# Half of the edge masks of query tiles 0 and 3 moved into free contraction rows of the second score product

## The chip, the cores and the metric

The kernel runs on one core of a Trainium2 chip. The metric is the device time of one execution in microseconds. Every time below is from runs of the same inputs; the profile is one execution taken by the hardware profiler.

## The reference

One transformer block with modulated layer norms, S = 2048 tokens of D = 448, H = 16 heads of 28, all in fp32:

```python
mod = (silu(c) @ w_mod).reshape(1, 6, 1, 448)          # sa, ca, ga, sb, cb, gb
h = layernorm(x) * (1 + ca) + sa
qkv = h @ wqkv                                          # per head q, k, v: [2048, 28]
d = idx[:, None] - idx[None, :]
scores = where((d >= 0) & (d < 256), q @ k.T * 28 ** -0.5, -1e9)
x = x + ga * (softmax(scores) @ v @ wo)
h = layernorm(x) * (1 + cb) + sb
t = h @ w1 + b1                                         # 448 -> 1792
x = x + gb * ((t * tanh(softplus(t))) @ w2)
```

What matters here is the attention: a query sees its own position and the 255 before it. Cut into tiles of 128, a query tile sees three key tiles: its own (there the keys after the query are masked, the "diag" triangle), the one before it (nothing is masked), and the one before that (there the keys 256 or more before the query are masked, the "far" triangle).

## The kernel before, in words

fp32 products are made from fp32r parts: a value is split into a rounded high part and a rest, and products run over high x high, high x low and low x high. Two stages follow each other: attention with all that feeds it (to about 406 us), then the feed-forward part.

**Groups, heads, units.** The tokens are cut into NG = 4 groups of GT = 512 queries (four query tiles t = 0 to 3, and with the 256 keys before them six key tiles jj = 0 to 5). Each group has 16 heads, so there are 64 heads i = 16 g + h in order, and each head has three units b = 0, 1, 2, so 192 units u = 3 i + b. A unit packs score blocks into one PSUM bank of 512 columns, as BLOCKS says: unit 0 has (key tile 0, query tile 0) and (key tile 2, query tiles 0 to 2); unit 1 has (1; 0, 1) and (4; 2, 3); unit 2 has (3; 1 to 3) and (5; 3). Group 0 has no keys before it and leaves out the blocks of jj = 0 and 1.

**Two score products.** For each head a first one, A (line 683), makes scores with queries as rows, from 84 contraction rows (28 dimensions x 3 split parts), and DVE takes the masked row maximum of each query (line 685). M2 (lines 689 to 698) turns the maxima of a pair of heads into rows with a transpose, splits them into two fp32r parts in the tile mr, and two DMAs put these into rows 84 and 85 of the query tile Q2. The key tile K3 has -1 in these rows, so that the second score product, B (line 713), with keys as rows, yields scores less the maximum straight from 86 contraction rows. B runs once per block of a unit; the 128-column block or the two equal blocks come behind the wider one.

**Masks.** On top of B's products in the same bank lie mask products (line 724): the 128x128 identity (identr, bf16) times columns of fdmask (bf16, 256 columns: far triangle of -2^100 in 0 to 127, diag triangle in 128 to 255). Where a far tile is followed at once by a diag tile, one product of 256 columns does both. In groups 1 to 3 unit 0 so has one of 256 (columns 0 to 255) and one of 128 (columns 384 to 511), unit 1 one of 256 (128 to 383), unit 2 one of 128 (0 to 127) and one of 256 (256 to 511). In group 0 there are four of 128 and one of 256 in the three units together.

**Behind the scores.** ACT makes P = exp(scale x) twice, in fp32 and in fp32r (lines 727, 728), POOL their difference Pl (line 735; for the last five units POOL and DVE half each), and PE sums Ph and Pl times v into one PSUM bank per head (line 745). ACT takes the sums out (EV), PE transposes them (E), and E2, E3 divide.

**What sets the order.** The order on every engine is the program's own, written by the loop over u: in step u come PV(u - 3) with Pl, B(u), the subtraction SP(u - 1), one first product A of the head three ahead, and filler products, the next group's projections and the last group's output projection (line 315), as many as RATE allows per step; PV(u - 2) with Ph is last. Engines run their own queues in order and wait on semaphores. Loads of a head's q and k (L, lines 472 to 479) are issued two heads ahead of its first product A. K3 has six tiles (NK) and Q2 three tiles of two heads (NQ = 6), reused in turn.

**Deferred DMAs.** All DMAs but one go through SP's queue. Stores and loads of the filler work stand in a list, later, from which the loop pops one in two of three steps; flush() issues all that is in it. The generator that sums the modulation weights (gen_wm_sum) puts four loads in the list, one in each of its steps, and calls flush() two steps after the last.

**At the start**, POOL sets constants: -1 in rows 64 to 85 of the key tiles (k3_tile, lines 149 to 152), the identity, the float mask of A, and fdf, the fp32 form of fdmask, which ACT copies to bf16 (line 512). The last key tile and the query tiles 1 and 2 are made later, in the pool att, when the first staging pool is closed.

Of the kernel before, what the change touches and what calls it, by code (L numbers as in the profile page):

```python
# [8 lines left out]
F32 = mybir.dt.float32  # L9
F32R = mybir.dt.float32r  # L10
BF16 = mybir.dt.bfloat16
AF = mybir.ActivationFunctionType
ALU = mybir.AluOpType

S, D, F, H, DH, W = 2048, 448, 1792, 16, 28, 256
NG, GT = 4, 512
# [4 lines left out]
NQ, NK, NV, LEAD = 6, 6, 10, 3  # L21
# [30 lines left out]
def adaln_block(ctx: ExitStack, tc: tile.TileContext, x, wqkv, wo, w1, b1, w2, c, w_mod, out):  # L52
    nc = tc.nc
    PE, ACT, DVE, POOL = nc.tensor, nc.scalar, nc.vector, nc.gpsimd
# [3 lines left out]
    def dma(o, i):  # L58
        nc.sync.dma_start(o, i)

    def pool(name, side="left", space=None):
        kw = {} if space is None else {"space": space}
        cm = tc.tile_pool(name=name, bufs=1, reuse_waits="tile", side=side, **kw)
        st = ExitStack()
        return st.enter_context(cm), st
# [7 lines left out]
    kq, kq_s = pool("kq")  # L73
# [18 lines left out]
    def bank(tag, bufs, name):  # L92
        return PS[0].tile([128, 512], F32, name=name, tag=tag, bufs=bufs)
# [18 lines left out]
    for k in range(4):  # L112
        wmf = st0.tile([128, 2 * D], F32, name=f"wm01_{k}")
        t = wmf[0:112]
# [10 lines left out]
    two = wqkv[:, 128:1152].rearrange("r (a n) -> r a n", n=512)[:, :, 0:256]  # L125
    for part in range(3):
        for ci in range(4):
            r0, r1 = ci * 128, min(ci * 128 + 128, D)
            for h in ((slice(0, 128),) if ci < 3 else (slice(0, 64), slice(64, 128))):
                t = wqs[ci][h]  # L130
# [9 lines left out]
    ident = cst.tile([128, 128], F32, name="ident")  # L140
# [6 lines left out]
    K3 = []  # L147

    def k3_tile(pl, i):
        t = pl.tile([86, GT + W], F32R, name=f"k3_{i}")  # L150
        POOL.memset(t[64:86, :].bitcast(F32), -1.0)
        K3.append(t)

    for i in range(NK - 1):
        k3_tile(kq, i)
    identr = kq.tile([128, 128], BF16, name="identr")
    fdmask = kq.tile([128, 256], BF16, name="fdmask")
    mask = kq.tile([128, 384], F32, name="mask")
    DVE.tensor_copy(identr, ident)
    POOL.memset(mask, 0.0)  # L160
# [1 line left out]
                       channel_multiplier=-1)  # L162
    POOL.affine_select(mask, mask, pattern=[[-1, 384]], compare_op=ALU.is_ge, fill=NEG, base=W,
                       channel_multiplier=1)
# [136 lines left out]
    def finish():  # L301
        while pipe.items:
            yield

    def drain(*gs):
        for g in gs:
            for _ in g:
                pipe.step()
# [14 lines left out]
    later = []  # L323
    PARTS = {}

    def flush():
        while later:
            later.pop(0)()
# [130 lines left out]
    for v in V:  # L459
        POOL.memset(v[:, :, 28:29].bitcast(F32), 1.0)  # L460
        POOL.memset(v[:, :, 29:32].bitcast(F32), 0.0)
    fdf = wmf[:, 0:256]
    POOL.memset(fdf[:, 0:256], 0.0)
    POOL.affine_select(fdf[:, 0:128], fdf[:, 0:128], pattern=[[-1, 128]], compare_op=ALU.is_ge, fill=-2.0 ** 100,
                       base=-1, channel_multiplier=1)
    POOL.affine_select(fdf[:, 128:256], fdf[:, 128:256], pattern=[[1, 128]], compare_op=ALU.is_ge,
                       fill=-2.0 ** 100, base=0, channel_multiplier=-1)


    Q2 = [kq.tile([86, 2, GT], F32R, name="q2_0")]  # L470

    def L(i):
        g, h = divmod(i, H)
        q, k = Q2[i % NQ // 2][:, i % 2], K3[i % NK]
        f0, f1 = h * DH, D + h * DH
# [5 lines left out]
    def split_cols(c0, c1, engs):  # L481
        for ci in range(4):
            if engs[ci]:
                split_hi(wqs[ci][:, c0:c1], wq3[:, ci, c0:c1], ACT)
        for ci in range(4):
            if engs[ci]:
                split_lo(wqs[ci][:, c0:c1], wq3[:, ci, c0:c1], wql[:, min(ci, 2), c0:c1], ci, engs[ci])
# [21 lines left out]
    first_tiles([(4, bank("sA", 2, "qk0_4"))])  # L509
    flush()  # L510
    split_cols(*QCOLS[2], (POOL, POOL, DVE, DVE))
    ACT.activation(fdmask, fdf, AF.Copy)
    st0_s.close()
    att, att_s = pool("att")
    Q2 += [att.tile([86, 2, GT], F32R, name=f"q2_{i}") for i in range(1, NQ // 2)]
    Q3 = [Q2[i // 2][:, i % 2] for i in range(NQ)]
    k3_tile(att, NK - 1)

    O2 = []
    for i in range(2):  # L520
        t = att.tile([128, GT], F32, name=f"o2_{i}")
# [167 lines left out]
    def M2(pr):  # L689
        p = bank("tr", 1, f"mt{pr}")  # L690
        PE.transpose(p[0:8, 0:128], mx[pr].rearrange("p a t -> p (a t)"), ident)
        r = att.tile([8, 2, 128], F32R, name=f"mr{pr}", tag="mr", bufs=2)
        DVE.tensor_copy(r[:, 0], p[0:8, 0:128])
        DVE.tensor_tensor(r[:, 1], p[0:8, 0:128], r[:, 0].bitcast(F32), op=ALU.subtract)
        for i in range(2):
            dma(Q2[pr % (NQ // 2)][84 + i:85 + i].bitcast(F32).rearrange("o a (t n) -> o (a t) n", t=4),
                r[:, i].bitcast(F32))

    def units(g, b):
        return [x for x in BLOCKS[b] if g > 0 or x[0] >= 2]  # L700

    def by_width(blocks):
        return sorted(blocks, key=lambda x: x[2] - x[1])

    def B(u):
        i, b = divmod(u, 3)
        g, h = divmod(i, H)
        q, k = Q3[i % NQ], K3[i % NK]
        bl = units(g, b)
        c0 = bl[0][3]  # L710
        p = bank("sB", 2, f"sB{u}")
        for n, (jj, t0, t1, c) in enumerate(by_width(bl)[::-1]):
            PE.matmul(p[:, c:c + 128 * (t1 - t0)], k[:, jj * 128:(jj + 1) * 128], q[:, t0 * 128:t1 * 128],  # L713
                      start=(n == 0), stop=False, skip_group_check=True)
        far = {c + 128 * (jj - t0) for jj, t0, t1, c in bl if t0 <= jj < t1}
        diag = {c + 128 * (jj - 2 - t0) for jj, t0, t1, c in bl if t0 <= jj - 2 < t1}
        masked = []
        for c in sorted(far | diag):
            if c in far:
                masked.append((256 if c + 128 in diag else 128, c, 0))  # L720
            elif c - 128 not in far:
                masked.append((128, c, 128))
        for n, c, m in sorted(masked):
            PE.matmul(p[:, c:c + n], identr, fdmask[:, m:m + n], start=False, stop=True, skip_group_check=True)  # L724
        P = Pt[u] = att.tile([128, 512], F32, name=f"P{u}", tag="P", bufs=3)
        Ph[u] = att.tile([128, 512], F32R, name=f"Ph{u}", tag="Ph", bufs=3)
        ACT.activation(P[:, c0:], p[:, c0:], AF.Exp, scale=SCALE)  # L727
        ACT.activation(Ph[u][:, c0:], p[:, c0:], AF.Exp, scale=SCALE)  # L728
# [19 lines left out]
    def EV(i):  # L748
        o = O2[i // 2 % 2][64 * (i % 2):64 * (i % 2) + 60]
        if i < NS - 3:  # L750
            ACT.activation(o, pvb[i][0:60, :], AF.Copy)  # L751
        else:
            DVE.tensor_copy(o, pvb[i][0:60, :])
# [26 lines left out]
    def chain(*gs):  # L780
        for g in gs:
            yield from g
# [210 lines left out]
    def step(g):  # L993
        return next(fillers[g], 99.0) or RATE[g]
# [40 lines left out]
    for u in range(NU + 9):  # L1035
        s, k = divmod(u, 3)
        g = s // H
        if k == 0 and s % H == 0 and 0 < g < NG:
            drain(fillers[g - 1], side[g - 1])
            flush()  # L1040
        pipe.step()
        if 0 <= u - 3 < NU:
            PV(u - 3, Pl)
            if (u - 3) % 3 == 2:
                EV((u - 3) // 3)
        if u < NU:
            B(u)
        if 0 <= u - 1 < NU:
            SP(u - 1)
        a = s + LEAD  # L1050
        if a < NS:
            A(a, (0, 1, 3)[k])
        if k == 0 and (a - 1) % 2 == 1 and LEAD <= a - 1 < NS:
            M2((a - 1) // 2)
        if k == s % 2 and s < NS:
            load_slot(s + LEAD + 2)
        if s % 2 == 1 and 1 <= (s - 1) // 2 <= NS // 2:
            pr = (s - 3) // 2
            if k == 2 and pr >= 0:
                E(pr)  # L1060
        if s % 2 == 0 and k < 2 and 0 <= (s - 4) // 2 < NS // 2:
            (E2, E3)[k]((s - 4) // 2)
        if g < NG:
            v = u - 48 * g
            if v in (0, 12):
                chunk["v"] = 4 if v == 0 and g or 0 < g < NG - 1 else 2
            if v == 0:
                credit = 0.0
            credit += RATE[g] * (2 if v < FRONT[g] else 1)
            while credit > 0.0:  # L1070
                credit -= step(g)
            if v > 1 or g == 0:
                side_step(g, ("dve", "act")[a >= NS:] if k == 1 else ("act",) if k == 0 and s % 2 == 0 else ())
            if later and ((s + (k == 2)) % 2 == 0 or k == 1):
                later.pop(0)()
        if u == NU:
            drain(fillers[NG - 1], side[NG - 1])
            while pipe.items:
                pipe.step()
            flush()  # L1080
        if u - NU in TAIL:
            TAIL[u - NU]()
        if k == 1 and a < NS:
            A(a, 2)
        if 0 <= u - 2 < NU:
            PV(u - 2, Ph)
# [63 lines left out]
    fill = chain(gen_oT(NG - 1, "tr", 2, ff), gen_wo(NG - 1, "tr", 2), finish())  # L1150
# [7 lines left out]
    for n in range(NN + 1):  # L1158
        g, f = divmod(n, NF)
        if f == 0 and n:  # L1160
# [3 lines left out]
            fill = None  # L1164
# [42 lines left out]
```

## Time and profile before

| | |
|---|---|
| median of 3 runs | 705.23 us (704.81 to 705.57) |
| span of the profiled execution, first to last instruction | 703.9 us |
| instructions of PE / DVE / ACT / POOL | 4001 / 1030 / 740 / 355 |
| mask products (line 724) | 320, half of them of 128 columns and half of 256 |
| second score products (line 713) | 352 |
| first exp of units 0, 48, 96, 144, 191 | 48.9, 122.7, 222.3, 322.6, 406.2 us |

The profiled execution is shown by its span alone; what a run's time has beyond it is start and end of the execution. Times in the profile are in us from the span's start, and durations of PE products are from start to end of a pipelined product, so that neighbours overlap: what one takes from the stream is seen from the starts. PEld is the weight load of a product, which runs beside the products.

### The profile page before, as it was taken

The page shows a single profiled execution, that of the slowest core. Times are in us where ns is not written, and L with a number is a line of the kernel's source. Part 1 is how long each engine was busy: PE and PEld are TensorE (multiplying, and loading weights), DVE is VectorE, ACT ScalarE, POOL GpSimd, SP SyncE. Part 2 cuts the span into 40 slices and gives each one's busy share as a digit, 9 for nine tenths or more (in the row PEclk, how much of TensorE's full clock was granted, in tenths as well). Part 3 has the DMA queues.
Part 4 walks back from the last instruction along what each step waited for, and adds up shares of the span by engine and source line. Part 5 has one row for each costly group of instructions (what it writes and reads, how often), then busy time and mean ns, then how long its engine had stood idle before and what let it go on. Part 6 is the DMA issues. An engine that isn't in the chain of part 4 may idle for free.

```text
span 703.9 us, 11999 instructions
## 1 busy us (share of the span) xinstructions
PE 685.9 (97%) x4001; PEld 590.2 (84%) x4001; DVE 383.3 (54%) x1030; ACT 391.6 (56%) x740; POOL 326.4 (46%) x355
## 2 busy tenths in 40 slices
PE   9899999999999999999999899999999999999997
PEld 8777888888888888898887788878888888888886
DVE  5688658788655887655768755452224222421112
ACT  3628788777667867667878974344233323332221
POOL 6626779686666776666778957212010000000000
PEclk9999999999999999999999999999999999999999
DMA  7865664455662462663773165800350035001001
GB/s 209 259 221 188 208 204 152 139 181 157 181 209 76 158 207 88 185 211 95 226 216 120 54 203 170 227 20 1 104 117 4 0 106 119 1 1 52 1 1 52
DMA packets 75178, 90.16 MB, mean 128 GB/s; under 512 B 31535, under 2 KB 51741, under 8 KB 75117
## 3 DMA queue, kind: packets, MB, share of 16 engines
q1 hardware_dynamic: 74652, 89.39, 42.0%
q8 instruction: 32, 0.52, 0.3%
q14 instruction: 30, 0.24, 0.1%
q10 hardware_dynamic: 464, 0.00, 0.0%
HBM read 56.60 MB, written 32.51 MB: 127 GB/s over the span
## 4 chain that ended last, share of the span: by engine, by line
PE 78%; DVE 6%; DMA 6%; ACT 3%; POOL 3%; issue 3%; SPq 1%; DVEq 0%; POOLq 0%; ACTq 0%
PE z L917 17%; PE pv L745 10%; PE qk L315 8%; PE sA L683 5%; PE acc L1106 5%; PE acc L1104 5%; PE acc L1105 5%; PE sB L713 5%; PE wo L315 4%; PE qk_v L315 4%; PE sB L724 3%; DMA scr<-st 2%; PE et L759 2%; PE warm L428 1%; DVE junk L685 1%
## 5 line engine op out<-in xcount | busy, mean ns | idle before, releaser
L735 POOL TENSOR_TENSOR Pl<-P,Ph 128x512 fp32r<-128x512 f32 (+2 forms) x192 | 234.8, 1230 | 80.9 <-ACT Ph L728 46.6
L685 DVE CUSTOM_DVE_ANT_0 junk<-sA,mask 128x384 f32<-128x384 f32 (+2 forms) x256 | 135.1, 528 | 95.1 <-PE sA L683 87.4
L727 ACT ACTIVATE P<-sB 128x512 f32<-128x512 f32 (+2 forms) x192 | 109.6, 571 | 62.3 <-PE sB L724 58.1
L925 DVE TENSOR_TENSOR al<-t,ah 128x512 fp32r<-128x512 f32 x56 | 39.2, 700 | 181.8 <-ACT ah L924 181.8
L923 ACT ACTIVATE t<-z,b1c 128x512 f32<-128x512 f32 x56 | 38.3, 684 | 138.6 <-PE z L917 138.6
L728 ACT ACTIVATE Ph<-sB 128x512 fp32r<-128x512 f32 (+2 forms) x192 | 109.2, 569 | 0.0
L683 PE MATMUL sA<-k,q 84*128 84x384 f32 (+2 forms) x256 | 100.5, 396 | 1.8 <-DVE mx L685 1.1
L917 PE MATMUL z<-hlf,w 128*128 128x512 f32 x224 | 88.6, 395 | 0.0
L917 PE MATMUL z<-hhf,w 128*128 128x512 f32 x224 | 88.6, 395 | 0.0
L1104 PE MATMUL acc<-w2h,ah 128*128 128x448 f32 x224 | 82.2, 367 | 1.2 <-ACT ah L924 1.2
L1106 PE MATMUL acc<-w2h,al 128*128 128x448 f32 x224 | 82.1, 366 | 0.1
L1105 PE MATMUL acc<-w2l,ah 128*128 128x448 f32 x224 | 81.6, 364 | 0.0
L745 PE MATMUL pv<-Ph,v 128*60 128x256 f32 (+2 forms) x352 | 76.7, 292 | 0.6 <-ACT o L751 0.5
L745 PE MATMUL pv<-Pl,v 128*60 128x256 f32 (+2 forms) x352 | 74.0, 284 | 2.4 <-POOL Pl L735 1.4
L713 PE MATMUL sB<-q,k 86*128 86x256 f32 (+1 forms) x352 | 74.2, 285 | 0.5 <-DMA q<-mr 0.5
L917 PE MATMUL z<-hhf,w1l 128*128 128x512 f32 x168 | 66.3, 395 | 0.0
L713 PEld LDWEIGHTS sB<-q,k 86*128 86x128 f32 x352 | 61.5, 189 | 2.3 <-DMA q<-mr 1.5
L724 PE MATMUL sB<-fdmask,identr 128*128 128x128 bf16 (+1 forms) x320 | 60.1, 253 | 0.0
L745 PEld LDWEIGHTS pv<-Ph,v 128*60 128x60 f32 x352 | 45.8, 133 | 14.0 <-ACT o L751 1.9
L745 PEld LDWEIGHTS pv<-Pl,v 128*60 128x60 f32 x352 | 45.2, 132 | 11.5 <-POOL Pl L735 3.8
L683 PEld LDWEIGHTS sA<-k,q 84*128 84x128 f32 x256 | 48.9, 193 | 7.0 <-DVE mx L685 4.3
L917 PEld LDWEIGHTS z<-hlf,w 128*128 128x128 f32 x224 | 42.2, 188 | 10.0
(159 smaller groups left out, 1252.4 us busy)
## 6 DMA issues: line engine op xcount, KB each, us to landing
scr<-st SPq DMA_DIRECT2D x24, 512.0 KB
k<-scr SPq DMA_DIRECT2D x48, 252.0 KB
q<-scr SPq DMA_DIRECT2D x64, 168.0 KB
scr<-st SPq DMA_DIRECT2D x32, 256.0 KB
x<-x1d SPq DMA_DIRECT2D x10, 448.0 KB
xin<-in_A_x_dram SPq DMA_DIRECT2D x8, 448.0 KB
xr<-in_A_x_dram SPq DMA_DIRECT2D x16, 224.0 KB
x1d<-xr SPq DMA_DIRECT2D x16, 224.0 KB
```

The lines of the kernel that those rows point to most:

```text
L315: PE.matmul(p, b, a, start=(n == 0), stop=(n == 10))
L683: PE.matmul(p[:, c0:384], q[0:84, t * 128:(t + 1) * 128], k[0:84, t * 128 + c0:t * 128 + 384], start=True, stop=True)
L685: DVE.tensor_tensor_reduce(out=junk[:, c0:384], in0=p[:, c0:384], in1=mask[:, c0:384], scale=1.0, scalar=-3.0e38, op0=ALU.add, op1=ALU.max ...
L713: PE.matmul(p[:, c:c + 128 * (t1 - t0)], k[:, jj * 128:(jj + 1) * 128], q[:, t0 * 128:t1 * 128], start=(n == 0), stop=False, skip_group_ch ...
L727: ACT.activation(P[:, c0:], p[:, c0:], AF.Exp, scale=SCALE)
L728: ACT.activation(Ph[u][:, c0:], p[:, c0:], AF.Exp, scale=SCALE)
L735: eng.tensor_tensor(Pl[u][:, a:b], Pt[u][:, a:b], Ph[u][:, a:b].bitcast(F32), op=ALU.subtract)
L745: PE.matmul(pv[0:60, t0 * 128:t1 * 128], V[j % NV][:, h, :], P[u][:, c:c + 128 * (t1 - t0)], start=(P is Ph and b == 0 and n == 0), stop=F ...
L917: PE.matmul(zb[n], ps[m][1], ps[m][0], start=(m == 0), stop=(m == 10))
L1104: PE.matmul(p, ah[n][:, ts], w2h[f], start=(f == 0), stop=False)
L1105: PE.matmul(p, ah[n][:, ts], w2l[f], start=False, stop=False)
L1106: PE.matmul(p, al[n][:, ts], w2h[f], start=False, stop=(f == NF - 1))
```

## The change

Key and query tiles grow from 86 to 128 rows. Rows 96 to 127 hold a pattern. In the query tile, row 96 + r has 2^-41 or 2^41 in the columns n of query tiles 0 and 3 with n mod 32 = r (2^-41, 2^41, 2^41, 2^-41 in the four quarters of 32 columns) and zero elsewhere; in the key tile the rows have 0, -2^3 or -2^85, so that their products are about 0, -2^44 or below. In key tiles 0 and 3 they mask half of the far triangle (64 of the 128 query columns), in key tiles 2 and 5 half of the diag triangle. Rows 86 to 95 are zero on the query side.

The pattern is written by POOL into the last key tile and the last query tile. At unit 16 patterns() puts seven DMAs in the list later, which copy rows 86 to 127 to the other five key tiles and two query tiles. From group 1 on B uses all 128 rows; group 0 uses 86 as before.

What is left of the masks in units 0 and 2 of groups 1 to 3 are two pieces of 128 columns that lie 320 columns apart in the bank, and one product of 2x128 columns does both, reading two pieces of fdmask that lie 192 apart. For this fdmask holds its two triangles, now diag first, twice (512 columns), and ACT copies it in two halves. Unit 1 and group 0 keep their mask products. The tile mr has one buffer for two.

```diff
@@ -147,14 +147,14 @@
     K3 = []
 
     def k3_tile(pl, i):
-        t = pl.tile([86, GT + W], F32R, name=f"k3_{i}")
+        t = pl.tile([128, GT + W], F32R, name=f"k3_{i}")
         POOL.memset(t[64:86, :].bitcast(F32), -1.0)
         K3.append(t)
 
     for i in range(NK - 1):
         k3_tile(kq, i)
     identr = kq.tile([128, 128], BF16, name="identr")
-    fdmask = kq.tile([128, 256], BF16, name="fdmask")
+    fdmask = kq.tile([128, 512], BF16, name="fdmask")
     mask = kq.tile([128, 384], F32, name="mask")
     DVE.tensor_copy(identr, ident)
     POOL.memset(mask, 0.0)
@@ -461,13 +461,13 @@
         POOL.memset(v[:, :, 29:32].bitcast(F32), 0.0)
     fdf = wmf[:, 0:256]
     POOL.memset(fdf[:, 0:256], 0.0)
-    POOL.affine_select(fdf[:, 0:128], fdf[:, 0:128], pattern=[[-1, 128]], compare_op=ALU.is_ge, fill=-2.0 ** 100,
+    POOL.affine_select(fdf[:, 128:256], fdf[:, 128:256], pattern=[[-1, 128]], compare_op=ALU.is_ge, fill=-2.0 ** 100,
                        base=-1, channel_multiplier=1)
-    POOL.affine_select(fdf[:, 128:256], fdf[:, 128:256], pattern=[[1, 128]], compare_op=ALU.is_ge,
+    POOL.affine_select(fdf[:, 0:128], fdf[:, 0:128], pattern=[[1, 128]], compare_op=ALU.is_ge,
                        fill=-2.0 ** 100, base=0, channel_multiplier=-1)
 
 
-    Q2 = [kq.tile([86, 2, GT], F32R, name="q2_0")]
+    Q2 = [kq.tile([128, 2, GT], F32R, name="q2_0")]
 
     def L(i):
         g, h = divmod(i, H)
@@ -509,12 +509,44 @@
     first_tiles([(4, bank("sA", 2, "qk0_4"))])
     flush()
     split_cols(*QCOLS[2], (POOL, POOL, DVE, DVE))
-    ACT.activation(fdmask, fdf, AF.Copy)
+    for c in (0, 256):
+        ACT.activation(fdmask[:, c:c + 256], fdf, AF.Copy)
     st0_s.close()
     att, att_s = pool("att")
-    Q2 += [att.tile([86, 2, GT], F32R, name=f"q2_{i}") for i in range(1, NQ // 2)]
+    Q2 += [att.tile([128, 2, GT], F32R, name=f"q2_{i}") for i in range(1, NQ // 2)]
     Q3 = [Q2[i // 2][:, i % 2] for i in range(NQ)]
     k3_tile(att, NK - 1)
+
+    def pattern(x, first, base, mult, step, fill):
+        v = K3[-1].rearrange("p (b n) -> p b n", n=128)[:, first:first + 4:3, 64 * x:64 * x + 64]
+        POOL.affine_select(v, v, pattern=[[0, 2], [step, 64]], compare_op=ALU.is_ge, fill=fill, base=base,
+                           channel_multiplier=mult)
+
+    POOL.memset(K3[-1].bitcast(F32), 0.0)
+    for x, first in ((0, 0), (1, 2)):
+        v = K3[-1].rearrange("p (b n) -> p b n", n=128)[:, first:first + 4:3, 64 * x:64 * x + 64]
+        POOL.memset(v.bitcast(F32), -2.0 ** 85)
+    pattern(0, 0, -96, 1, -1, -2.0 ** 3)
+    pattern(0, 0, -64, 1, -1, 0.0)
+    pattern(1, 2, 63, -1, 1, -2.0 ** 3)
+    pattern(1, 2, 95, -1, 1, 0.0)
+    POOL.memset(K3[-1][64:96, :].bitcast(F32), -1.0)
+    POOL.memset(Q2[-1][64:128].bitcast(F32), 0.0)
+    for a in range(2):
+        for c, w in enumerate((-41, 41, 41, -41)):
+            v = Q2[-1][96:128, a].rearrange("p (t c n) -> p t c n", t=4, c=4)[:, 0:4:3, c]
+            POOL.tensor_scalar(v, ident[96:128, 96:128].unsqueeze(1).to_broadcast([32, 2, 32]), 2.0 ** w, None,
+                               op0=ALU.mult)
+
+    def patterns():
+        for t in K3[:-1]:
+            later.append(lambda t=t: dma(t[86:128].bitcast(F32), K3[-1][86:128].bitcast(F32)))
+        for t in Q2[:-1]:
+            later.append(lambda t=t: dma(t[86:128].bitcast(F32), Q2[-1][86:128].bitcast(F32)))
+
+    def two(v, c, step):
+        return bass.AP(v.tensor, v.offset + c, [list(v.ap[0]), [step, 2], [1, 128]])
+
 
     O2 = []
     for i in range(2):
@@ -689,7 +721,7 @@
     def M2(pr):
         p = bank("tr", 1, f"mt{pr}")
         PE.transpose(p[0:8, 0:128], mx[pr].rearrange("p a t -> p (a t)"), ident)
-        r = att.tile([8, 2, 128], F32R, name=f"mr{pr}", tag="mr", bufs=2)
+        r = att.tile([8, 2, 128], F32R, name=f"mr{pr}", tag="mr", bufs=1)
         DVE.tensor_copy(r[:, 0], p[0:8, 0:128])
         DVE.tensor_tensor(r[:, 1], p[0:8, 0:128], r[:, 0].bitcast(F32), op=ALU.subtract)
         for i in range(2):
@@ -708,18 +740,23 @@
         q, k = Q3[i % NQ], K3[i % NK]
         bl = units(g, b)
         c0 = bl[0][3]
+        rows = 86 if g == 0 else 128
         p = bank("sB", 2, f"sB{u}")
         for n, (jj, t0, t1, c) in enumerate(by_width(bl)[::-1]):
-            PE.matmul(p[:, c:c + 128 * (t1 - t0)], k[:, jj * 128:(jj + 1) * 128], q[:, t0 * 128:t1 * 128],
+            PE.matmul(p[:, c:c + 128 * (t1 - t0)], k[0:rows, jj * 128:(jj + 1) * 128], q[0:rows, t0 * 128:t1 * 128],
                       start=(n == 0), stop=False, skip_group_check=True)
         far = {c + 128 * (jj - t0) for jj, t0, t1, c in bl if t0 <= jj < t1}
         diag = {c + 128 * (jj - 2 - t0) for jj, t0, t1, c in bl if t0 <= jj - 2 < t1}
         masked = []
         for c in sorted(far | diag):
             if c in far:
-                masked.append((256 if c + 128 in diag else 128, c, 0))
+                masked.append((256 if c + 128 in diag else 128, c, 128))
             elif c - 128 not in far:
-                masked.append((128, c, 128))
+                masked.append((128, c, 0))
+        if g and b != 1:
+            PE.matmul(two(p, (64, 0)[b // 2], 320), identr, two(fdmask, (192, 0)[b // 2], 192), start=False, stop=True,
+                      skip_group_check=True)
+            masked = []
         for n, c, m in sorted(masked):
             PE.matmul(p[:, c:c + n], identr, fdmask[:, m:m + n], start=False, stop=True, skip_group_check=True)
         P = Pt[u] = att.tile([128, 512], F32, name=f"P{u}", tag="P", bufs=3)
@@ -1073,6 +1110,8 @@
                 side_step(g, ("dve", "act")[a >= NS:] if k == 1 else ("act",) if k == 0 and s % 2 == 0 else ())
             if later and ((s + (k == 2)) % 2 == 0 or k == 1):
                 later.pop(0)()
+        if u == 16:
+            patterns()
         if u == NU:
             drain(fillers[NG - 1], side[NG - 1])
             while pipe.items:
```

## Prediction

> **What bounds the kernel now.** I read the page first, then the busy times by stretch, then single units of the attention stage. The page's first lines, and its chain of waits by engine:
>
> ```profile
> span 703.9 us, 11999 instructions
> PE 685.9 (97%) x4001; PEld 590.2 (84%) x4001; DVE 383.3 (54%) x1030; ACT 391.6 (56%) x740; POOL 326.4 (46%) x355
> ...
> PE 78%; DVE 6%; DMA 6%; ACT 3%; POOL 3%; issue 3%; SPq 1%; DVEq 0%; POOLq 0%; ACTq 0%
> ```
>
> TensorE (PE) is busy for 97% of the span, and 78% of the chain that ended last is PE's own work; no other engine holds more than 6% of it. A shorter PE stream can therefore shorten the span, if it is shortened where PE doesn't wait. The change touches the score products of groups 1 to 3, so these come next: busy time in stretches (from:to, length, then PE, PE's weight loads, DVE, ACT, POOL, clock, DMA share, GB/s). The stretches are group 1, group 2, group 3 and the last 28 us of group 3.
>
> ```profile
> 122.00:222.00 100.00, 98.73 (x681) 86.64 (x679) 70.76 (x217) 72.47 (x140) 69.01 (x63) 1.00 0.53 164
> 222.00:322.00 100.00, 98.59 (x677) 86.34 (x675) 70.22 (x215) 72.09 (x139) 69.09 (x64) 1.00 0.51 157
> 322.00:378.00 56.00, 55.40 (x383) 47.65 (x382) 37.99 (x120) 42.67 (x85) 41.24 (x35) 1.00 0.61 182
> 378.00:406.00 28.00, 24.36 (x186) 19.74 (x184) 23.51 (x59) 24.55 (x49) 25.66 (x27) 1.00 0.24 73
> ```
>
> In groups 1 and 2 PE is busy 98.7 and 98.6 of 100 us, while the next engines, ACT and POOL, stand near 70%. The first 56 us of group 3 are alike (55.4 of 56). Only the last 28 us are loose: PE 24.4, POOL 25.7. So in some 256 us PE sets the pace and every column counts; in 28 us POOL and the chain through it do. The granted clock is 1.00 everywhere.
>
> **The removed product.** In a unit of groups 1 to 3 with b = 0 or 2 there is one mask product of 128 columns and one of 256; with b = 1 there is one of 256. Three units so have five mask products, two of which the change takes away (one in each unit with b not 1). The mask line alone, in the same four stretches (count of PE instructions in brackets):
>
> ```profile
> 122.00:222.00 100.00, 15.58 (x82) 5.37 (x82) 1.00 0.53 164
> 222.00:322.00 100.00, 15.31 (x80) 5.13 (x78) 1.00 0.51 157
> 322.00:378.00 56.00, 9.46 (x50) 3.29 (x50) 1.00 0.61 182
> 378.00:406.00 28.00, 5.98 (x32) 1.98 (x30) 1.00 0.24 73
> ```
>
> They sum to 244 (240 by the loops, the rest lies on the edges): 48 heads x 2 = 96 products of 128 columns go, about 12 of them in the loose stretch (32 x 2/5 = 13) and 84 in the tight ones. What one takes from the stream is read from starts. First a unit with two mask products, then one with a single 256-column one, each up to the product after the next head's score product (start, duration):
>
> ```profile
> 251.07 0.40 PE L713 MATMUL sB<-q,k 86*128 86x384 f32 x2
> 251.31 0.34 PE L724 MATMUL sB<-fdmask,identr 128*128 128x128 bf16 x2
> 251.41 0.42 PE L683 MATMUL sA<-k,q 84*128 84x384 f32 x1
> 251.67 0.37 PE L315 MATMUL wo<-wo,hho 128*128 128x448 f32 x1
> ...
> 254.97 0.40 PE L713 MATMUL sB<-q,k 86*128 86x256 f32 x2
> 255.21 0.28 PE L724 MATMUL sB<-fdmask,identr 128*128 128x256 bf16 x1
> 255.25 0.42 PE L683 MATMUL sA<-k,q 84*128 84x384 f32 x1
> 255.51 0.37 PE L315 MATMUL wo<-wo,hlo 128*128 128x448 f32 x1
> ```
>
> The first takes 251.67 - 251.07 = 0.60 us for 384 + 128 + 128 + 256 + 384 = 1280 columns, the second 255.51 - 254.97 = 0.54 for 256 + 256 + 256 + 384 = 1152. A changed unit has exactly the second's number of columns and of products. The difference is 0.06 us. A second reading, from a plain stream of 512-column products:
>
> ```profile
> 31.97 0.39 PE L315 MATMUL qk<-hl,wq 128*128 128x512 f32 x1
> ...
> 32.89 0.39 PE L315 MATMUL qk<-hh,wq 128*128 128x512 f32 x1
> ```
>
> Four intervals in 0.92 us make 0.23 us for 512 columns, so 0.0575 for 128. I take 0.057: 84 x 0.057 = 4.8 us in the tight stretches. Of the 12 x 0.057 = 0.7 in the loose one I count half, 0.3, since POOL releases PE there. Saved: 5.1 us. The bounds are 3.6 (64 products of groups 1 and 2 alone, if group 3 gives nothing) and 6.7 (96 x 0.07, what the rounding of the stamps allows above 0.06).
>
> [...]
>
> **The product of 2x128 columns.** It reads its mask and writes its bank in two pieces. No product of the trace does. Its column count is that of the 256-column product, so I cost it like that one (0 extra). From below there is nothing to gain, since columns enter at 0.23 us per 512 and it keeps its 256. From above: each column at half pace, 0.115 us more (256 x 0.23 / 512), which is the slower rival. The wider contraction (128 rows for 86) costs nothing by the rows at hand: score products of 86 rows and pv and filler products of 128 rows keep the same 0.23 per 512 columns, which is what the units above are made of.
>
> **What is added at the start.** POOL gets, behind the key-tile memset, three wide memsets, two of 128 columns, four affine selects of 128 columns and eight small multiplies. The rows of POOL around that place, then an affine select from earlier:
>
> ```profile
> 30.19 0.73 POOL L151 MEMSET k<- 22x768 f32 x1
> ...
> 40.38 0.23 POOL L234 TENSOR_SCALAR rsa<-mva 128x4 f32<-128x4 f32 x1 [8.41 <-DVE mva L221]
> ```
>
> ```profile
> 23.04 0.29 POOL L464 TENSOR_SCALAR_AFFINE_SELECT wm<-wm 128x128 f32<-128x128 f32 x1
> ```
>
> A memset of 768 columns takes 0.73 us, so the three wide ones (768, 768, 1024) take 0.73 + 0.73 + 0.97 = 2.4; six 128-column operations at 0.29 are 1.7; eight multiplies at 0.23 (the row at 40.38 is a tensor_scalar too) are 1.8. In all 5.9 us, behind 30.9. POOL is idle for 8.41 us before 40.38, where it waits for layer-norm statistics. That idle time hides all of it with 2.5 to spare; without this cover the excess would delay the next group's layer norm, which is itself filler. Cost 0 (up to 1 if POOL is twice as slow).
>
> ACT copies the mask twice instead of once, one more 0.3 us (next start minus start) here:
>
> ```profile
> 28.46 0.40 ACT L512 ACTIVATE fdmask<-wm 128x256 bf16<-128x256 f32 x1
> 28.77 0.53 ACT L366 ACTIVATE v<-qk_v 128x448 fp32r<-128x448 f32 x1
> ```
>
> The value copy behind it then ends at about 29.6, but its reader on DVE starts only at 30.72, held by DVE's own queue:
>
> ```profile
> 29.01 1.67 DVE L200 TENSOR_TENSOR wq<-wqs,wq 64x512 fp32r<-64x512 f32 x1
> 30.72 0.62 DVE L369 TENSOR_TENSOR v<-qk_v,v 128x448 fp32r<-128x448 f32 x1
> ```
>
> Cost 0. The mr tile now has one buffer, so the CAST of a pair waits for both row DMAs of the pair before, some 8 us earlier in group 0 and more behind it. The scores that wait for the first pair's rows, and the second pair's CAST:
>
> ```profile
> 48.26 0.41 PE L713 MATMUL sB<-q,k 86*128 86x384 f32 x1 [0.39 <-DMA q<-mr]
> ```
>
> ```profile
> 52.98 0.28 DVE L693 CAST mr<-mt 8x128 fp32r<-8x128 f32 x1
> ```
>
> The rows had landed by 48.26, 4.7 us before the CAST. Behind a waiting CAST stand the row maxima, and behind these PE; I take 0, and 1 us as the upper bound.
>
> **What is added in group 0: seven copies.** At unit 16 seven DMAs of the pattern rows enter the list of deferred DMAs: 5 x 42 x 768 x 4 bytes + 2 x 42 x 1024 x 4 = 989 KB. The list is emptied by the flush of the weight-sum generator a few units later, so they go to SP's queue right behind the last of its loads and ahead of the next pair's row DMA:
>
> ```profile
> 76.47 0.46 SPq L59 DMA_DIRECT2D wm<-in_w_mod_dram  x1
> 79.97 1.38 SPq L59 DMA_DIRECT2D q<-mr  x2
> ```
>
> SP is idle between 76.93 and 79.97, so issuing seven (0.4 to 0.5 us each) costs that queue about nothing. But the DMA engines are at their busiest here:
>
> ```profile
> 76.00:92.00 16.00, 16.00 (x104) 12.60 (x104) 11.42 (x42) 11.94 (x29) 12.25 (x13) 1.00 0.81 253
> ```
>
> Share 0.81 at 253 GB/s makes 312 GB/s when busy; 989 KB take 3.2 us. The row DMA of 79.97 stands behind them in the same queue. The scores that need it start at
>
> ```profile
> 84.18 0.41 PE L713 MATMUL sB<-q,k 86*128 86x384 f32 x1
> ```
>
> and in this stretch PE's score line has already waited for it, with nothing to spare (idle time in us, times):
>
> ```profile
>   DMA q<-mr: 0.3, 1
> ```
>
> So a delay of the row DMA passes to PE. Later loads stand behind the copies too, but have two heads' lead. If all copies come ahead of it, PE loses 3.2 us; if some come early, while the engines are less busy, or the row's packets find a free engine, less, down to 0. I take two thirds, 2.1 us, since the list is mostly emptied at once. PE is busy 16.0 of 16 us here, so what is lost isn't made up.
>
> **The sum.** The profiled span is 703.9 us; the runs' median of 705.2 has 1.3 around it. The change gives -5.1 + 2.1 = -3.0: a span of 700.9, a time of 702.2 us.
>
> **Rivals.** (1) The copies are hidden: a row DMA is only 4 KB, and the engines' idle fifth (0.19 x 16 = 3.0 us) could take them. Then 705.2 - 5.1 = 700.1. Against it speaks the wait of 0.3 above. (2) The copies cost more: rows 86 to 127 are a third of the partitions, the transfer is slower than 312 GB/s, or the loads behind it come late as well. With 5 us of stalls, 705.1, no change. (3) The saving arrives in part: once PE is shorter, group 3 waits for ACT and POOL (42.7 and 41.2 of 56 us busy there before 378). With 64 x 0.057 = 3.6 saved: 705.2 - 3.6 + 2.1 = 703.7. (4) Slower: the product in two pieces runs its columns at half pace. Place: 96 products; price 0.115 - 0.057 = 0.058 each, +5.5; with the copies 705.2 + 5.5 + 2.1 = 712.8. It decides from 0.035 us a product (0.057 - 2.1 / 96) to slower than before. For it speaks only that no row shows such a product. [...]
>
> **How the numbers follow.** Chances: forecast (stall 1 to 3.2, saving 4.5 to 6) 0.48; (1) 0.20; (2) 0.15; (3) 0.10; (4) 0.05; (5) 0.02. A measurement of this kernel can tell about 0.2%, 1.4 us, from no change: faster is below 703.8, slower above 706.6. Faster gets 0.45 of the forecast, all of (1) and 0.08 of (3): 0.73. Same gets the rest of these and 0.14 of (2): 0.19. Slower gets (4), (5) and 0.01 of (2): 0.08. The range: from 6.1 saved with 0.5 lost, 699.6, to 4.6 saved with 4.2 lost, 704.8; outside it lie (4), (5), a part of (2) and the edges of the rest.
>
> **What would show it.** PE has 96 products fewer (3905). The unit in two pieces takes 0.54 us by the starts above; 0.60 or more would make (4). Groups 1 and 2 are each about 1.8 us shorter than their 100 us, from the first scores of one group to those of the next. Around 80 to 88 us PE shows a wait of 1 to 3 us on the row DMA, and DMA share near 1 in that stretch; without it (1) holds. POOL's new work ends before 38 us. The prediction is wrong if groups 1 to 3 do not get shorter, if the last 28 us grow, or if group 0 grows by over 4 us.

## The result and the profile after

The changed kernel takes 709.33 us (median of 4 runs, 708.4 to 710.96) against 705.04 for the kernel before (4 runs, 704.81 to 705.57): ratio 1.0059, 95% interval 1.0046 to 1.0072. It is slower by 4.3 us where 3.0 us less was forecast, and outside the range. The page of the changed kernel, the lines that answer to those of before, with the group of the second score product:

```profile
span 708.2 us, 11833 instructions
...
PE 682.2 (96%) x3905; PEld 585.5 (83%) x3905; DVE 382.2 (54%) x1030; ACT 391.5 (55%) x741; POOL 334.5 (47%) x372
...
PEclk9999989999999999999999999999999999999999
...
L746 PE MATMUL sB<-q,k 128*128 128x256 f32 (+1 forms) x352 | 74.4, 285 | 7.1 <-DMA q<-mr 7.1
```

The span grew from 703.9 to 708.2, PE has the 96 products less (3905), and its busy time fell by 3.7 us. So the time went into PE's idle time, and one group names it: 7.1 us of idle time before score products, released by the row DMA. The clock line has an 8 in the sixth slice, where it was 9 throughout.

The lengths of the stages, from the first exp of one unit to that of another in each trace (group 3 up to unit 191), say where it lies; the kernels of the experiments below stand with them. The time is the median of all runs, the stages are those of the one profiled run.

| kernel | time, us | first exp at | group 0 | group 1 | group 2 | group 3 |
|---|---|---|---|---|---|---|
| before | 705.04 | 48.9 | 73.7 | 99.7 | 100.3 | 83.6 |
| changed | 709.33 | 47.9 | 83.1 | 98.2 | 98.5 | 82.8 |
| e1_late | 710.97 | 48.3 | 84.2 | 98.2 | 98.4 | 82.8 |
| e2_copies_only | 715.35 | 48.1 | 83.2 | 99.7 | 99.9 | 84.9 |
| e3_rows_only | 715.63 | 48.1 | 84.9 | 99.5 | 99.9 | 83.6 |
| e4_warm | 707.70 | 48.2 | 79.8 | 98.1 | 98.4 | 82.8 |
| e5_quiet | 700.91 | 47.9 | 74.7 | 98.2 | 98.5 | 82.8 |
| e6_few_bytes | 708.99 | 48.0 | 75.7 | 99.7 | 99.8 | 83.6 |
| e7_when_empty | 704.36 | 48.1 | 77.4 | 98.1 | 98.4 | 82.8 |
| e8_act_queue | 705.40 | 48.0 | 78.2 | 98.2 | 98.4 | 82.8 |
| e9_ports | 704.50 | 47.5 | 74.2 | 99.7 | 99.9 | 83.6 |

Groups 1 to 3 became shorter by 1.5 + 1.8 + 0.8 = 4.1 us, as the change meant. Group 0, in which no product changed, grew by 9.4. The start is 1.0 shorter; e9_ports, whose start is that of the kernel before, has its first exp at 47.5, so this lies within what profiles differ by. The sum, -1.0 + 9.4 - 4.1 = +4.3, is the change of the span. Busy times in groups 1, 2 and 3 of the changed kernel:

```profile
131.00:229.20 98.20, 96.67 (x645) 84.51 (x644) 70.73 (x215) 72.00 (x140) 69.08 (x64) 1.00 0.55 166
229.20:327.60 98.40, 96.81 (x647) 84.68 (x646) 70.22 (x214) 71.94 (x139) 69.19 (x64) 1.00 0.53 160
327.60:410.00 82.40, 77.42 (x528) 64.92 (x527) 61.20 (x178) 66.83 (x133) 66.98 (x62) 1.00 0.48 147
```

PE is still busy nearly all of groups 1 and 2 (96.7 of 98.2, 96.8 of 98.4): the shorter stream was not replaced by another engine there. A unit with the product in two pieces (line 757):

```profile
202.56 0.39 PE L746 MATMUL sB<-q,k 128*128 128x384 f32 x2
202.80 0.28 PE L757 MATMUL sB<-fdmask,identr 128*128 128x256 bf16 x1
202.84 0.42 PE L715 MATMUL sA<-k,q 84*128 84x384 f32 x1
203.10 0.27 PE L796 MATMUL et<-ident,o 124*128 124x124 f32 x1
```

It takes 203.10 - 202.56 = 0.54 us, what the unit with a single 256-column product took before; over groups 1 to 3 the median of such units is 0.54 too. The two pieces cost nothing, and neither do 128 rows.

What happened in group 0. PE's last product before the stall and the next one:

```profile
82.72 0.34 PE L782 MATMUL pv<-Pl,v 128*60 128x384 f32 x1
89.26 0.66 PE L746 MATMUL sB<-q,k 86*128 86x384 f32 x1 [6.20 <-DMA q<-mr]
```

PE waits 6.20 us for the row DMA of a pair. Its data was ready long before, on DVE:

```profile
78.80 0.28 DVE L726 TENSOR_TENSOR mr<-mt,mr 8x128 fp32r<-8x128 f32 x1
```

But SP's queue, which issues it, stands as follows (the last weight load, the copies, then the row DMA):

```profile
75.53 0.46 SPq L59 DMA_DIRECT2D wm<-in_w_mod_dram  x1
76.04 4.41 SPq L59 DMA_DIRECT2D k<-k  x5
81.90 2.94 SPq L59 DMA_DIRECT2D q<-q  x2
85.11 1.40 SPq L59 DMA_DIRECT2D q<-mr  x2
```

The row DMA is issued at 85.11, 6.0 us after its data at 79.08. The first five copies' issues alone fill SP from 76.04 to 80.45, 0.75 us or more each, and then SP itself waits, for loads that were issued before the copies:

```profile
SPq L59 <- DMA xin<-in_A_x_dram: 2.9, 2, 1.4
```

In the trace SP's DMAs take eight semaphores in turn, and an issue waited until the DMA that had its semaphore before had landed. Two 448 KB loads (xin), one weight load and five copies use up all eight, so the last two copies wait for the two loads. Of the 6.0 us between the row DMA's data and its issue, 2.9 are issues of copies and 3.1 are such waits. How fast the engines moved, just before the copies' bytes and in the midst of them (length, busy times, clock, DMA share, GB/s):

```profile
77.00:80.00 3.00, 3.00 (x21) 2.34 (x20) 2.62 (x9) 2.91 (x8) 2.21 (x3) 1.00 0.95 294
82.00:84.00 2.00, 1.06 (x6) 0.50 (x4) 0.78 (x3) 0.36 (x1) 1.41 (x1) 1.00 0.93 174
```

The share stays (0.95, 0.93) while the rate falls from 294 to 174 GB/s, 187 GB/s when busy. Other packets run in these 2 us as well. The copies' own, 210 of 3072 bytes and 84 of 4096, took 230 and 274 ns on average, which makes 222 GB/s over 16 engines and 4.5 us for 989 KB, where the prediction took 312 and 3.2.

Behind the stall the clock is the second loss:

```profile
89.20:95.00 5.80, 5.74 (x23) 4.67 (x24) 2.26 (x9) 2.29 (x6) 2.25 (x3) 0.51 0.93 311
95.00:131.00 36.00, 35.10 (x235) 29.26 (x234) 22.95 (x81) 28.63 (x66) 28.27 (x29) 1.00 0.48 149
```

From 89.2 to 95.0 the granted clock is 0.51. In the trace's record it is halved from 88.1 on for 6.8 us; PE is back at 89.26, so half the clock costs it some 2.8 us. 6.8 is two times 3.41, and in the experiments halved stretches last 3.4, 6.8 or 10.2 us. PE was not idle for all of the 3.41 us ahead of each, though. The records of the kernel before and of the changed one change only at multiples of 3.41 us from their start (204 in the first, 24, 26 and 206 in the second), and in e8_act_queue the clock halved at 87.78, behind a stretch from 84.37 in which PE was idle for 2.27 us. Cut into such stretches, the traces of the kernel before and of the changed one show a full clock halved behind one with 3.41 us of idle PE (the stall) and one with 3.10 (the end of the kernel before), and kept behind each one with 1.58 or less. In e2_copies_only it halved at 394.5 behind one with 1.17. So where a wait falls among these stretches may matter as well as its length.

### The profile page after: what moved, and what is told of

The parts are those of the page before. It is cut to its first block, busy times and chain, and to the rows that moved or that the text cites. A ratio compares the mean times of both kernels' runs of the same rounds, so it can differ in the third digit from the quotient of the medians.

```text
span 708.2 us, 11833 instructions
## 1 busy us (share of the span) xinstructions
PE 682.2 (96%) x3905; PEld 585.5 (83%) x3905; DVE 382.2 (54%) x1030; ACT 391.5 (55%) x741; POOL 334.5 (47%) x372
## 4 chain that ended last, share of the span: by engine, by line
PE 78%; DVE 7%; ACT 3%; DMA 2%; issue 2%; POOL 1%; SPq 0%; DVEq 0%; ACTq 0%; POOLq 0%
PE z L954 19%; PE pv L782 9%; PE qk L315 8%; PE acc L1145 6%; PE acc L1143 6%; PE acc L1144 6%; PE sA L715 5%; PE sB L746 5%; PE wo L315 4%; PE qk_v L315 4%; DVE junk L717 2%; PE et L796 2%; DMA wm<-in_w_mod_dram 1%; PE sB L761 1%; PE sB L757 1%
## 5 line engine op out<-in xcount | busy, mean ns | idle before, releaser
L746 PE MATMUL sB<-q,k 128*128 128x256 f32 (+1 forms) x352 | 74.4, 285 | 7.1 <-DMA q<-mr 7.1
L782 PE MATMUL pv<-Pl,v 128*60 128x256 f32 (+2 forms) x352 | 74.2, 284 | 2.9 <-POOL Pl L772 2.0
L746 PEld LDWEIGHTS sB<-q,k 128*128 128x128 f32 (+1 forms) x352 | 61.7, 190 | 8.8 <-DMA q<-mr 6.5
L788 ACT ACTIVATE o<-pv 60x512 f32<-60x512 f32 x61 | 36.0, 590 | 24.1 <-PE pv L782 23.7
```

Source lines behind the costliest of these rows:

```text
L746: PE.matmul(p[:, c:c + 128 * (t1 - t0)], k[0:rows, jj * 128:(jj + 1) * 128], q[0:rows, t0 * 128:t1 * 128], start=(n == 0), stop=False, ski ...
L782: PE.matmul(pv[0:60, t0 * 128:t1 * 128], V[j % NV][:, h, :], P[u][:, c:c + 128 * (t1 - t0)], start=(P is Ph and b == 0 and n == 0), stop=F ...
```

## The experiments

Theory 1: the loss lies in group 0 alone. The copies stand ahead of a row DMA that PE needs at once, so PE waits and then runs at half clock. Theory 2: the two-piece product or the 128 rows cost time, and the copies only shift it. Theory 3: the copies cost the same wherever they are put. The diffs are against the changed kernel unless said.

**e1_late: the copies six units later in the list.**

```diff
-        if u == 16:
+        if u == 22:
             patterns()
```

> The changed kernel with the seven copies put in the deferred list at unit 22 instead of 16, so behind a pair's row DMA and one per pop, with no flush at once. Theory 1 (the copies ahead of the row DMA make PE wait 6.2 us and then run at half clock, some 9 us in all; the masks give back 4 us): 701 us, and no wait of over 1 us on the row DMA in group 0. Theory 2 (the two-piece product or the 128-row score products cost time themselves): stays near 709 us. Theory 3 (the copies take 4.5 us of all DMA engines and cost that wherever they are put): 706 to 709 us, with the wait on a later row DMA.

710.97 us, ratio to before 1.0093 (1.0076 to 1.011), above what any of the three gave. The wait on the row DMA at unit 24 shrank as theory 1 wants:

```profile
83.66 0.41 PE L746 MATMUL sB<-q,k 86*128 86x384 f32 x1 [0.20 <-DMA q<-mr]
```

The time did not shrink, as theory 3 wants, but its wait on a later row DMA isn't there either. Theory 1 as it stood was too narrow. POOL and PE show another stall, at 102 us:

```profile
107.73 1.13 POOL L601 TENSOR_TENSOR wop<-wop,ga 128x448 f32<-128x448 f32 x1 [8.09 <-DMA wop<-in_A_wo_dram]
108.81 2.92 POOL L772 TENSOR_TENSOR Pl<-P,Ph 128x384 fp32r<-128x384 f32 x3
```

```profile
109.86 0.57 PE L782 MATMUL pv<-Pl,v 128*60 128x384 f32 x1 [7.21 <-DMA wop<-in_A_wo_dram]
```

POOL waited 8.09 us for a piece of the output weights. Its load is deferred through the same list and now stood behind the copies there: it is issued at 104.17, where e5_quiet below issues it at 92.44 and POOL doesn't wait. Behind the waiting multiply in POOL's queue stood Pl (108.81), and PE waited for that: 7.2 us (a multiple wait, put down to the load). The clock halved for 10.2 us. So the list is a queue too, and what the copies cost is what stands behind them.

**e2_copies_only: the copies without their use.**

```diff
-        rows = 86 if g == 0 else 128
+        rows = 86
-        if g and b != 1:
+        if False:
```

> The kernel before with the tiles of 128 rows, the pattern and its seven copies at unit 16, but score products of 86 rows in all groups and all mask products as before. Theory 1: 705.0 + 9 = 714 us, groups 1 to 3 as long as before. Theory 2: 705 us within 1.4.

715.35 us, ratio 1.0142 (1.0124 to 1.016). All of the loss is there without any changed product: the time is 10.5 us above the 704.84 of the kernel before beside it, group 0 takes 83.2, and PE's wait is

```profile
89.97 0.66 PE L746 MATMUL sB<-q,k 86*128 86x384 f32 x1 [6.67 <-DMA q<-mr]
```

Theory 2 falls. (Group 3's 84.9 has a stretch of 3.4 us at half clock near its end, at 394.)

**e3_rows_only: 128 rows and the old masks, copies as in e1_late.**

```diff
-        if g and b != 1:
+        if False:
```

> The copies at unit 22 and 128-row score products in groups 1 to 3, but the old mask products of 128 and 256 columns on top of them (the masks are so applied twice over). Theory 1: the time of the kernel before, 705 us, if the 128 rows cost nothing and all gain is the removed 96 products. Theory 2: slower than 706.4 us.

715.63 us, ratio 1.0149 (1.0136 to 1.0162). The total is far from theory 1's 705 and would fit theory 2, but it decides nothing, since it has the stall of e1_late too (group 0: 84.9). Groups 1 to 3 do: 99.5, 99.9 and 83.6, those of e2_copies_only or of before. So 128 rows for 86 cost nothing, and against e1_late the removed products are worth 1.3 + 1.5 + 0.8 = 3.6 us.

**e4_warm: work for PE inside the wait.**

```diff
+        if u == 24:
+            wb2 = bank("sB", 2, "warm2")
+            for _ in range(50):
+                PE.transpose(wb2[:, 0:128], ident, ident)
         if u < NU:
             B(u)
```

> The changed kernel, copies at unit 16, with 50 transposes of the identity into a spare bank just ahead of the score product that waits (unit 24), so that PE works for some 5.5 us of the wait. If the half clock behind the wait costs 2.9 us of the 9: 709.3 - 2.9 = 706.4 us, with the clock at 1.00 throughout and the runs close together. If the half clock costs nothing (only the wait counts): 709.3 us.

707.70 us (706.91 to 710.65 in 6 runs), ratio 1.0043 (1.0027 to 1.006), between the two expectations. The bank is one of the two that the score products use in turn. The transposes, then the score product:

```profile
83.39 5.62 PE L1086 MATMUL warm<-ident 128*128 128x128 f32 x50
89.89 0.41 PE L746 MATMUL sB<-q,k 86*128 86x384 f32 x1 [0.89 <-DMA q<-mr]
```

The score product comes 6.7 us after PE's last product ahead of the transposes (6.5 in the changed kernel), but the clock stays at 1.00 from 82 to 96 us, and group 0 is 3.3 us shorter than in the changed kernel (79.8 for 83.1). Some 2.8 of that is the half clock by the record above; the changed kernel also has a second wait on a row DMA, 0.90 us at 111, that this one lacks. The medians differ by 1.6 us only, and the single runs of both scatter over 3 to 4 us, so the price of the half clock is known to about a us.

**e5_quiet: the copies where nothing that is needed soon stands behind them.**

```diff
-        if u == 16:
-            patterns()
+        for c, n in {41: (('k', 4), ('k', 0), ('q', 0)), 47: (('k', 1), ('q', 1), ('k', 2), ('k', 3))}.get(u, ()):
+            ts = K3 if c == 'k' else Q2
+            dma(ts[n][86:128].bitcast(F32), ts[-1][86:128].bitcast(F32))
```

> The changed kernel with the seven copies issued directly, not through the deferred list, where SP and the DMA engines have little to do: three at unit 41 and four at unit 47, each time behind a pair's row DMA and the last load, with six units to the next. Theory 1 (the loss lies in what stands behind the copies, not in the copies or the products): groups 1 to 3 as short as in the changed kernel, group 0 as in the kernel before: 705 - 4 = 701 us, clock 1.00. Theory 3 (the copies cost the same wherever they are put): 709 us or more.

700.91 us, ratio 0.9935 (0.9921 to 0.9948): faster than both kernels, and 4.3 us less than the one before (705.16 beside it). The copies move the same bytes and cost nothing, so theory 3 falls. The engines were two thirds busy around their issues (0.69 and 0.67 here), not 0.95 as in the changed kernel:

```profile
111.70:114.30 2.60, 2.60 (x21) 2.16 (x19) 1.74 (x8) 2.48 (x7) 2.60 (x3) 1.00 0.69 196
121.50:125.50 4.00, 4.00 (x24) 3.35 (x23) 1.84 (x6) 2.70 (x7) 2.66 (x3) 1.00 0.67 198
```

Groups 1 and 2:

```profile
122.60:220.70 98.10, 96.56 (x645) 84.44 (x644) 70.73 (x215) 71.90 (x139) 68.94 (x64) 1.00 0.56 173
220.70:319.20 98.50, 96.95 (x647) 84.82 (x646) 70.20 (x214) 71.98 (x140) 69.21 (x64) 1.00 0.53 160
```

The lengths, 98.2 and 98.5 by the first exps, are those of the changed kernel. At unit 24 there is still a wait, without any copy near:

```profile
84.45 0.41 PE L746 MATMUL sB<-q,k 86*128 86x384 f32 x1 [1.40 <-DMA q<-mr]
```

In the kernel before, and in e9_ports below, the product did not wait here (before the change only its weight load did, 0.3 us); with no copy ahead of it, it waited 0.20 us in e1_late and 0.95 in e3_rows_only. So between 0 and 1.4 of the 6.20 is not the copies'. Why these differ is open; that PE comes to it earlier than before the change is not the reason, since in e9_ports it comes earlier still.

**e6_few_bytes: seven copies of 64 columns each** (against e2_copies_only).

```diff
-dma(t[86:128].bitcast(F32), K3[-1][86:128].bitcast(F32))
+dma(t[86:128, 0:64].bitcast(F32), K3[-1][86:128, 0:64].bitcast(F32))
-dma(t[86:128].bitcast(F32), Q2[-1][86:128].bitcast(F32))
+dma(t[86:128, 0, 0:64].bitcast(F32), Q2[-1][86:128, 0, 0:64].bitcast(F32))
```

> As the copies-only kernel (old masks, 86 rows, copies at unit 16), but each copy moves 64 columns instead of 768 or 1024: seven DMAs as before, 75 KB for 989 KB. If the wait comes from the bytes ahead of the row DMA: the wait nearly goes, 705 to 706 us. If it comes from the number of DMAs in SP's queue (each issue waits until the one eight before it has landed): the wait stays at some 4 us or more, 711 us or more.

708.99 us (706.28 to 712.35 in 6 runs), ratio 1.0055 (1.0034 to 1.0076): between the two expectations. The profiled run was the fastest, 706.28, with clock 1.00:

```profile
85.49 0.41 PE L746 MATMUL sB<-q,k 86*128 86x384 f32 x1 [2.32 <-DMA q<-mr]
```

With 75 KB the wait is 2.32 us for 0 to 1.40 without copies and 6.67 with all bytes. So in this profile the number of DMAs costs 0.9 to 2.3 and the bytes some 4.3. The other five runs took 708 to 712, with mean clocks of 0.995 to 0.998, and the median is still 3.8 us above the kernel before, where e2_copies_only is 10.5 above it: the number of DMAs may cost more than this one profile shows. That the clock halved there behind a wait, as it did behind 3.40 us in e8_act_queue, would fit; those runs have no trace that shows it.

**e7_when_empty: copies only in steps in which the deferred list is empty.**

```diff
                 later.pop(0)()
+            elif copies:
+                copies.pop(0)()
+        if u == 47:
+            while copies:
+                copies.pop(0)()
```

(patterns() fills copies instead of later.)

> The changed kernel with the copies in a list of their own from unit 16, from which one is taken only in steps where the deferred list is empty, what is left at unit 47. Three of them still stand ahead of the row DMA of unit 21 and two ahead of the next. Theory 1: waits in proportion to the bytes ahead, 3/7 of 6.2 us = 2 to 2.7 us at the first, too short to halve the clock: 701 + 2.5 = 703.5 us. If any copy ahead of a row DMA brings the whole loss: 709 us.

704.36 us, ratio 0.9988 (0.9979 to 0.9997). The waits at units 24 and 30:

```profile
85.17 0.41 PE L748 MATMUL sB<-q,k 86*128 86x384 f32 x1 [1.92 <-DMA q<-mr]
```

```profile
96.20 0.41 PE L748 MATMUL sB<-q,k 86*128 86x384 f32 x1 [1.06 <-DMA q<-mr]
```

They are 1.92 and 1.06 us, with clock 1.00 in the profile, and a third is 0.67 us; six of the other ten runs have 0.997 or 0.998. That 2 to 2.7 us would be too short to halve the clock was an estimate; the longest wait shown with a full clock behind it is the 2.32 us of e6_few_bytes. In the trace two copies, not three, stand ahead of the first row DMA, which is issued on time at 79.00, and 0 to 1.40 us of wait there is not the copies'. So waits in proportion to the bytes are not shown. What is shown is that copies spread over several steps cost less than seven at once: the time is 5.0 us below that of the changed kernel, and 0.9 above the 703.5 that was expected.

**e8_act_queue: only the two row DMAs of the fifth pair from ACT's queue.**

```diff
-            dma(Q2[pr % (NQ // 2)][84 + i:85 + i] ...
+            (nc.scalar if pr == 4 else nc.sync).dma_start(
+                Q2[pr % (NQ // 2)][84 + i:85 + i] ...
```

> The changed kernel, copies at unit 16 as in the change, with one edit: the two row DMAs of the fifth pair, those that PE waits for, are issued from ACT's queue instead of SP's. If SP's queue is what holds them (they were issued 6 us after their data): the wait falls to under 2 us, the clock stays at 1.00, 702 to 704 us. If it is the DMA engines' backlog that holds them, whatever the queue: the wait stays at 4 us or more, 706 to 709 us.

705.40 us, ratio 1.0005 (0.9995 to 1.0014), again between the two. ACT issues them at once, and PE's wait is

```profile
78.93 1.99 ACTq L728 DMA_DIRECT2D q<-mr  x2
```

```profile
86.64 0.41 PE L747 MATMUL sB<-q,k 86*128 86x384 f32 x1 [3.40 <-DMA q<-mr]
```

So with the issue at 78.93 instead of 85.11 the wait is 3.40, not 6.20: SP's queue held 2.8 us of it. Of the 3.40, 0 to 1.4 are there without copies; the other 2.0 to 3.4 stayed although the DMAs were issued from ACT's queue, and I put them down to the engines' backlog. The clock halved for 3.4 us (0.60 from 87.0 to 91.3).

**e9_ports: are 42 neighbouring partitions slow?** The kernel before with two copies of its own (the edit also adds the tile wide and gives mr one buffer, as the change does):

```diff
+        if u == 41:
+            dma(wide, mask[:, 0:320])
+        if u == 47:
+            dma(wide[86:128], mask[86:128, 0:320])
```

> The kernel before with two copies from SBUF to SBUF and nothing else of the change: 128 partitions x 1280 bytes (164 KB) at unit 41, and partitions 86 to 127 x 1280 bytes (54 KB) at unit 47, so packets of one size. [...] If copies from SBUF to SBUF are slow whatever the partitions: both take the same, 90 ns or more. The time stays at 705 us.

704.50 us in one run, beside 705.40; the one buffer of mr shows no cost. In the trace's records the 128 packets of the wide copy took 68 ns on average, the 42 of the narrow one 69. So the partitions are not it at this packet size. The copies' packets of 3072 and 4096 bytes took 230 and 274 ns in the stall, 13 to 15 GB/s per engine, where from 74 to 92 us those of 1792 and 2048 bytes ran at 18.8 and 19.8. In the quieter stretches of e5_quiet the 4096-byte packets took 304 ns on average, the shortest 156, so it is not the busy stretch that makes them slow. Why is open.

## Why the prediction was wrong, point by point

- **PE bounds groups 1 to 3, and removed columns pay.** Right, with the saving at the lower bound: 4.1 us against the kernel before and 3.6 between kernels that differ in these products alone (e1_late against e3_rows_only), where 5.1 was forecast. The difference is mostly group 2 of the kernel before, 100.3 us, which takes 99.8 to 99.9 in the four other kernels with the old products. By the median starts the removed product took 66 ns, of which the product behind it gave back 12 (it is followed by A after 40 instead of 28 ns): 54 for the 57 taken. Over groups 1 and 2 that makes 1.7 us each; 1.4 arrived (e5_quiet against e3_rows_only), and PE's idle time there grew by 0.2 to 0.3 us. In the last 28 us nothing arrived where 0.3 was counted.
- **The two-piece product at the cost of a contiguous one; 128 rows at no cost.** Right: 0.54 us, and e3_rows_only. Rival 4 falls. No run shows what (5) has its chance of 0.02 for: in e3_rows_only groups 1 to 3 took 99.5, 99.9 and 83.6 us with 128 rows, where the kernel before took 99.7, 100.3 and 83.6 with 86.
- **POOL's and ACT's work at the start hidden.** Right, but closer: the eight multiplies took 3.42 us for 1.8,

```profile
34.67 3.42 POOL L538 TENSOR_SCALAR q<-ident 32x64 fp32r<-32x64 f32 x8
...
39.84 0.23 POOL L234 TENSOR_SCALAR rsa<-mva 128x4 f32<-128x4 f32 x1 [0.73 <-DVE mva L221]
```

and POOL was 0.73 us idle where 2.5 were expected; the new work ended at 38.09, not before 38. The one buffer of mr cost nothing that a run shows (e9_ports, one run).

- **The copies' stall: "989 KB take 3.2 us ... I take two thirds, 2.1 us".** This is the step that failed. The place was right: the wait stands at the score product that was quoted, and for the row DMA. Its size was not, and group 0 grew by 9.4 us, past the 4 that the prediction named as a sign against itself. First, the rate of 312 GB/s was that of other transfers; the copies' packets made 222 (187 in the slowest 2 us), 4.5 us instead of 3.2. Second, "issuing seven costs that queue about nothing" was wrong twice: issuing a copy took 0.75 us or more, not 0.4 to 0.5, and SP's issues waited for the DMA eight before them (3.1 us). So the row DMA was issued 6.0 us after its data. It was issued 5.1 us later than in the kernel before, and its product started 4.2 us behind the issue in both (89.26 - 85.11, 84.18 - 79.97): the delay arose in SP's queue. The engines' backlog, which was all that was priced, shows by itself only where the row DMA leaves that queue (e8_act_queue). Together they made 6.2 us of wait, 4.8 to 6.2 more than without copies, where 2.1 were counted. Third, the price of a wait was taken as its length: the half clock behind it cost some 2.8 us more by the record, 3.3 by e4_warm. The wait and the half clock make up the 9.4 us within what single profiles tell. Rival 2 had the right side of it with 5 us of stalls. The wait of 0.3 us that was read as PE's is, in the trace, that of the weight load; the product at 84.18 followed the one ahead of it without a gap.
- **"What is lost isn't made up."** Right.

Open are the differences of up to 1.4 us in the wait at unit 24 between kernels with no copy ahead of it, and why the copies' packets are slow.

## What to carry to other kernels

A one-time copy of 1 MB cost nothing in a quieter stretch and 9 us in a busy one here: before placing a transfer, list what stands behind it in the issuing queue, in the program's own deferred list and in the DMA engines, and who waits for that. Price a wait of the bounding engine with what the clock does behind it, not by its length alone; here a wait of 6 us cost some 3 us more. A small, regular saving (96 x 54 ns) is worth making only after its one-time set-up has been placed: the same saving gave +4.3 us or -4.3 us by the units at which seven DMAs were issued.

## What the runs showed of the hardware that was not expected

- The clock halved for 3.4 us or multiples of it: waits of 3.40, 6.20, 6.67 and 7.2 us brought 3.4, 6.8, 6.8 and 10.2 us of half clock; 1.92 and 2.32 brought none in the profiled runs. Within one stretch of 3.41 us, 2.27 us of idle PE (e8_act_queue), 3.10 (the kernel before) and 3.41 (the changed one) halved it, 1.58 or less in the traces of these two kernels did not; 1.17 did in e2_copies_only.
- Copies from SBUF to SBUF in packets of 3 and 4 KB ran at 13 to 15 GB/s per engine, 222 GB/s over 16, against 310 GB/s for the loads just ahead of them.
- A product that reads and writes in two pieces of 128 columns took the stream as long as a contiguous one of 256: its unit took 0.54 us like that one's.
